# A planned retention and MLP kernel: tile 7's q and k transposed by DMA, one more pair split, TensorE's order changed at the start

## The chip, the cores and the metric

The kernel runs on one core of one Trainium2 chip. The metric is the device time of one execution in microseconds (us), lower is better. The median of four runs of the kernel before is 216.2 us (215.89 to 217.82).

The engines are named as the profile does: PE is TensorE (PEld its weight loads), DVE is VectorE, ACT is ScalarE, POOL is GpSimd and SP is SyncE, which only issues DMAs here.

## The reference

There are 4 sequences of 768 steps with 8 heads of width 64. The first half is a recurrence per head with a decay gamma:

```
gamma = 1 - 2 ** (-5 - h)
for t in range(S):
    state = gamma * state + k[t] (outer) v[t]
    y[t]  = q[t] @ state / sqrt(D)
```

The heads of y are laid side by side, which gives x with 4 x 768 rows of 512. The second half is a normalization and a two-layer network with a residual:

```
xn  = (x - mean(x)) / sqrt(var(x) + 1e-6) * g_ln
out = x + max(xn @ w_ch1, 0) @ w_ch2        # w_ch1: 512 x 2048, w_ch2: 2048 x 512
```

Inputs and output are float32; the kernel computes its products in bf16.

## The kernel before, in words

The 3072 rows are cut into 24 tiles of 128 (`TILES`): tiles 0 to 3 are the first chunks of the four sequences, and then come the other five chunks of each sequence, 4 to 8, 9 to 13, 14 to 18, 19 to 23.

For each tile the recurrence is done chunk by chunk. Its q and k are needed with the head's width on the partitions, so they are transposed, and q is scaled (`trq`). There are two ways. A tile below `T0` is transposed on PE: `e_tk` (L403) and `e_tq` (L410) write four 128x128 blocks each into PSUM (`tp`), ACT copies k's out (`trk`), and DVE scales q's out of PSUM (L415). A tile from `T0` on has q and k loaded into one buffer `qk` (five of them), and SP issues one DMA that transposes both (`tr`, L425); DVE then scales q from SBUF (L432). The PE steps of a tile are: `e_pa` (L442), scores of q and k; DVE multiplies them by the decay mask (`asb`, L449); `e_py` (L461, L465), the state's part and the chunk's part of y; `e_pd` (L511), the chunk's addition to the state, from `vg` (v scaled, on POOL, L498), which DVE turns into the next `state` (L525). DVE takes mean and variance of y (L479, L480) and writes the normalized `xn` (L474), ACT copies y as the residual (`x_all`, L485).

For the network, xn is transposed: below `TX` on PE (L541, copied out by ACT, L188), else by DMA (L555). `GROUPS` says how many tiles share one first product: `e_m1` (L588) multiplies w1 blocks by 1, 2 or 4 tiles' xn (128, 256 or 512 columns), 16 row blocks in all, several in one step so that each step fills a 512-column PSUM tile (`mm`, two of them). ACT or DVE applies the maximum (`h`, L601, L603). `e_m2` (L625) makes the second product of a tile, 16 multiplications of 512 columns in four parts, and DVE adds the residual (`osb`, L633); SP stores it.

The order of everything is set by a small planner (`Plan`) while the kernel is built. Each step is added with an engine, an assumed length, a rank, the steps that it comes after, and the buffer that it takes; `lat` is an assumed extra delay until others see it, and `follows` puts it behind another step in the plan without using its result. `order()` picks again and again the step that can start earliest, then the lowest rank. What it yields is each engine's fixed instruction order; on the chip only that order and the semaphores count, not the planner's times. A changed number in the plan can thus move steps that are not named in the change. `fill` puts products of zeros (L649) into PE's planned gaps in the first 20 us of the plan. Loads are issued by POOL (L342 and L350), cast to bf16 on the way, in its planned order between its `vg` steps, and each load waits for the eighth before it.

The lines that matter here:

```
GROUPS = [1] * 6 + [2] * 5 + [4] * 2
T0, TX = 8, 8
gbm = a(PE, 1000, 2, c_gb, [grd, small2], ("mm", "g"), at=7600)
2800 if kind in "qkv" and j > 7 else 1400 if late(kind, j) else 250,
tk = a(PE, 230, r - 0.1, e_tk, [loaded["k", t], ident] + ([tq] if tq else []),
       ("tp", ("k", t)), [where["k", t]])
```

Of the kernel before, what the change touches and what calls it, by code (L numbers as in the profile page):

```python
# [14 lines left out]
PE, ACT, DVE, POOL, SP = range(5)  # L15
# [101 lines left out]
def kernel(  # L117
# [26 lines left out]
    NPAIR = H // 2  # L144
    TILES = [(b, 0) for b in range(B)] + [(b, c) for b in range(B) for c in range(1, C)]
    number = {bc: t for t, bc in enumerate(TILES)}
    GROUPS = [1] * 6 + [2] * 5 + [4] * 2
    NG = len(GROUPS)
    G0 = [sum(GROUPS[:g]) for g in range(NG)]
    GMAX = max(GROUPS)  # L150
    T0, TX = 8, 8

    buf_of = {g: divmod(G0[g], GMAX) for g in range(NG)}
    group_of = {G0[g] + i: (g, i) for g in range(NG) for i in range(GROUPS[g])}

# [27 lines left out]
    def take(pool, key, shape, dtype):  # L183
        held[pool, key] = pools[pool].tile(shape, dtype, name=pool, tag=pool)
        return held[pool, key]

    def evacuate(eng, dst, src):
        nc.scalar.copy(out=dst, in_=src) if eng == ACT else nc.vector.tensor_copy(out=dst, in_=src)  # L188
# [85 lines left out]
    a = plan.add  # L274
    small = a(DVE, 1450, -100, c_small)
    small2 = a(DVE, 200, -99, c_small2)
# [16 lines left out]
    def c_gb(eng):  # L293
# [2 lines left out]

    grd = a(SP, 390, -150, lambda eng: nc.sync.dma_start(
        out=grow[0:1, :], in_=moe_g_ln.rearrange("(o n) -> o n", o=1)), [small], lat=4500)
    gbm = a(PE, 1000, 2, c_gb, [grd, small2], ("mm", "g"), at=7600)
    gl = a(ACT, 600, -40, lambda eng: nc.scalar.copy(out=gb, in_=held["mm", "g"]), [gbm],  # L300
           uses=[("mm", "g")])

# [2 lines left out]
    loaded, where = {}, {}  # L305

    def tile_of(kind, t):
        if kind != "v" and t >= T0:
            return held["qk", t][:, "qk".index(kind)]
        return held[where[kind, t]]  # L310

    def load(kind, j, rank):
        takes, uses, follows = None, [], []
        if kind in "qkv":
            b, c = TILES[j]
            src = {"q": q, "k": k, "v": v}[kind][b].rearrange("h (c p) d -> c p h d", p=P)[c]
            ns, dma = 910, 900
            pair = kind != "v" and j >= T0
            name = "qk" if pair else kind + ("0" if c == 0 and kind != "q" else "sb")
            takes = where[kind, j] = (name, j)  # L320
            if pair and kind == "q":
                takes, uses, follows = None, [takes], [loaded["k", j]]

            if j == 0:

                def emit32(eng):
                    dst = take("osb", kind, [P, DM], FP32).rearrange("p (h d) -> p h d", d=D)
                    (nc.scalar if eng == ACT else nc.sync).dma_start(out=dst, in_=src)
                raw = a(ACT if kind == "q" else SP, 390, -200 + "kqv".index(kind), emit32, (),
                        ("osb", kind), (), 0, {"k": 3400, "q": 4000, "v": 4800}[kind])  # L330

                def emit(eng):
                    evacuate(eng, take(*takes, [P, H, D], BF16),
                             held["osb", kind].rearrange("p (h d) -> p h d", d=D))
                loaded[kind, j] = a({"k": {ACT: 620}, "q": {DVE: 490}, "v": {ACT: 620, DVE: 430}}[kind], 0, -60, emit,
                                    [raw], takes, [("osb", kind)])
                return

            def emit(eng):
                if takes:  # L340
                    take(*takes, [P, 2, H, D] if pair else [P, H, D], BF16)
                nc.gpsimd.dma_start(out=tile_of(kind, j), in_=src)  # L342
        else:
            s = slice(j * DM, (j + 1) * DM)
            o = slice(j * KO, (j + 1) * KO)
            src, dst = (w1_v[:, :, s], w1[:, :, s]) if kind == "w1" else (w2_v[:, o, :], w2[:, o, :])
            ns, dma = 820, 2450 if kind == "w1" else 2800

            def emit(eng):
                nc.gpsimd.dma_start(out=dst, in_=src)  # L350
        loaded[kind, j] = a(POOL, ns, rank, emit, (), takes, uses, dma,
                            2800 if kind in "qkv" and j > 7 else 1400 if late(kind, j) else 250,
                            follows=follows)

    def late(kind, j):
        return j > 2 if kind in "qkv" else kind == "w2" or j > 0
# [8 lines left out]
    for i, (x, j) in enumerate(seq):  # L365
        load(x, j, pool_rank.get(f"{x}_{j}" if x[0] == "w" else f"{x}{j}", 20 * i))
# [5 lines left out]
    for g in range(NG):  # L372
        for ho in range(HO):
            unit["1", g, ho] = u
            u += GROUPS[g] / 4
            if g >= 6 and (ho + 1) % (HO // GROUPS[g]) == 0 and behind:
                unit["2", behind.pop(0)] = u
# [7 lines left out]
    for t in range(NT):  # L385
        g, i = group_of[t]
# [5 lines left out]
    for t in range(NT):  # L392
        b, c = TILES[t]
        r = rank_of[t]
        g, i4 = group_of[t]
# [3 lines left out]
        if t < T0:  # L399
            def e_tk(eng, t=t):  # L400
                p = take("tp", ("k", t), [P, NPAIR, P], BF16)
                for i in range(NPAIR):
                    nc.tensor.transpose(p[:, i, :], tile_of("k", t)[:, 2 * i:2 * i + 2, :], idn)  # L403
            tk = a(PE, 230, r - 0.1, e_tk, [loaded["k", t], ident] + ([tq] if tq else []),
                   ("tp", ("k", t)), [where["k", t]])

            def e_tq(eng, t=t):
                p = take("tp", ("q", t), [P, NPAIR, P], BF16)
                for i in range(NPAIR):
                    nc.tensor.transpose(p[:, i, :], tile_of("q", t)[:, 2 * i:2 * i + 2, :], idn)  # L410
            tq = a(PE, 230, r, e_tq, [loaded["q", t], ident, tk], ("tp", ("q", t)),
                   [where["q", t]])

            def e_eq(eng, t=t):
                nc.vector.tensor_tensor(out=take("trq", t, [P, NPAIR, P], BF16),  # L415
                                        in0=held["tp", ("q", t)], in1=qsc, op=ALU.mult)
            eq = a(DVE, 430, r, e_eq, [tq, qscd] + ([eq] if eq else []), ("trq", t), [("tp", ("q", t))])

            def e_ek(eng, t=t):
                evacuate(eng, take("trk", t, [P, NPAIR, P], BF16), held["tp", ("k", t)])  # L420
            ek = a({ACT: 590}, 0, r, e_ek, [tk], ("trk", t), [("tp", ("k", t))])
            kt = ("trk", t)
        else:
            def e_tr(eng, t=t):
                nc.sync.dma_start_transpose(  # L425
                    out=take("tr", t, [P, H, P], BF16),
                    in_=held["qk", t].rearrange("p a h d -> p (a h d)"))
            ek = a(SP, 1230, r - 16, e_tr, [loaded["k", t], loaded["q", t]], ("tr", t), [("qk", t)],
                   1500, 5000)

            def e_eq(eng, t=t):
                nc.vector.tensor_tensor(out=take("trq", t, [P, NPAIR, P], BF16),  # L432
                                        in0=held["tr", t][:, 0:NPAIR, :], in1=qsc, op=ALU.mult)
            eq = a(DVE, 490, r, e_eq, [ek, qscd, eq, am], ("trq", t), [("tr", t)])
            kt = ("tr", t)
# [10 lines left out]
        pat = a(PE, 430, r + 1.2, e_pa, [eq, ek], ("pa", t), [("trq", t), kt])  # L446
# [43 lines left out]
        if c > 0:  # L490
            for cc in ([0, 1] if c == 1 else [c]):
                if cc == C - 1:
                    continue
                j = number[b, cc]

                def e_vg(eng, j=j, cc=cc):
# [7 lines left out]
                        follows=[loaded["q", j + 2]] if T0 <= j < NT - 2 else [])  # L504
# [46 lines left out]
        else:  # L551
            def e_ex(eng, t=t, xb=xb, xi=xi):
                if xi == 0:
# [4 lines left out]
                      follows=[ex[t - 1]] if xi else [])  # L558
# [53 lines left out]
    for t, cols in [(t, slice(0, DM)) for t in range(NT - 1)] + [  # L612
            (NT - 1, slice(0, DM - P)), (NT - 1, slice(DM - P, DM))]:
        g, i4 = group_of[t]
# [70 lines left out]
```

## Time and profile before

| | |
|---|---|
| median of four runs | 216.2 us |
| the profiled execution | 217.66 us |
| its span | 215.9 us |
| PE busy | 205.7 us |
| DVE busy | 122.5 us |
| ACT busy | 82.0 us |
| POOL busy | 89.5 us |
| granted TensorE clock | 0.999 |
| read from and written to HBM | 27.27 MB, 6.29 MB |

The span is the time from the first to the last instruction that the profiler saw; the execution's own time is 1.76 us longer. Busy time of an engine is the time in which it worked on at least one instruction. The page gives groups of equal instructions, with the mean length of one. A product's length there is the time through the array, and products overlap, so the spacing of two is less than the mean length; the chain and the timeline give spacings. The chain follows the work that ended last back from the end: at each step to what released it. In the timeline the idle time ahead of an instruction stands in brackets with what ended it.

### The profile page before, as it was taken

Reading aid. Unit: us, or ns where it says so; the run is one execution under the profiler, and the core shown is the slowest. Engines: PE = TensorE matmul, PEld = TensorE weight load, DVE = VectorE, ACT = ScalarE, POOL = GpSimd, SP = SyncE. Lnnn points to the kernel's source line nnn. Section 1 sums busy time; section 2 is a strip of 40 time slices with the busy share of each in tenths; the row PEclk is TensorE's granted clock in tenths of the full one; section 3 lists DMA queues with packets and bytes.
Section 4 is the critical chain, followed back from the end, with each engine's and each line's share of the span. In section 5 each row is a group of like instructions: output and inputs, shape, how many; then the busy total and the mean of one; then the engine's idle time right before and its main releaser. Section 6 shows DMA issues by size and latency. Waiting matters only on the chain.

```text
span 215.9 us, 4578 instructions
## 1 busy us (share of the span) xinstructions
PE 205.7 (95%) x1889; PEld 132.5 (61%) x1911; DVE 122.5 (57%) x233; ACT 82.0 (38%) x153; POOL 89.5 (41%) x105
## 2 busy tenths in 40 slices
PE   7888999999999997899999999999999999999994
PEld 2557999986855645687778775544444444444442
DVE  7695878985148999995776586697011111012121
ACT  5455656674421113255546541136540044430000
POOL 8987779966961839876602930000000000000000
PEclk9999999999999999999999999999999999999999
DMA  7999999999999999999999996412111111011212
GB/s 141 179 179 180 180 157 191 207 163 147 146 158 175 225 140 212 168 162 133 145 149 164 148 182 117 125 24 76 24 49 49 49 49 52 0 49 49 97 52 97
DMA packets 108326, 26.91 MB, mean 125 GB/s; under 512 B 101009, under 2 KB 105361, under 8 KB 108306
## 3 DMA queue, kind: packets, MB, share of 16 engines
q0 software_dynamic: 75984, 13.24, 87.2%
q1 hardware_dynamic: 31138, 13.05, 32.0%
q10 hardware_dynamic: 1184, 0.33, 0.7%
q8 instruction: 15, 0.25, 0.5%
q14 instruction: 5, 0.04, 0.1%
HBM read 27.27 MB, written 6.29 MB: 155 GB/s over the span
## 4 chain that ended last, share of the span: by engine, by line
PE 82%; DVE 9%; DMA 3%; issue 2%; POOL 2%; ACT 1%; POOLq 0%
PE mm L588 38%; PE tp L625 33%; DMA k<-in_k_dram 3%; PE pa L442 3%; DVE asb L449 2%; PE py L465 2%; DVE trq L432 2%; PE py L461 2%; PE pd L511 2%; DVE state L525 1%; DVE osb L633 1%; DVE bns L479 1%; PE tp L541 1%; PE tp L403 1%; PE tp L410 1%
## 5 line engine op out<-in xcount | busy, mean ns | idle before, releaser
L588 PE MATMUL mm<-xnt,w 128*128 128x128 bf16 (+2 forms) x832 | 93.5, 264 | 0.9 <-ACT h L601 0.9
L625 PE MATMUL tp<-w,h 128*128 128x512 bf16 (+2 forms) x380 | 86.5, 370 | 1.5 <-issue 0.6
L588 PEld LDWEIGHTS <-w 128*128 128x128 bf16 x832 | 65.0, 98 | 21.8 <-issue 1.3
L601 ACT ACTIVATE h<-mm 128x512 bf16<-128x512 f32 x89 | 52.7, 597 | 62.5 <-PE mm L588 49.4
L625 PEld LDWEIGHTS <-h 128*128 128x128 bf16 x400 | 37.3, 98 | 39.7
L633 DVE SCALAR_TENSOR_TENSOR osb<-tp,rstd,x_all 128x512 f32<-128x512 f32 (+2 forms) x25 | 18.2, 728 | 58.8 <-PE tp L625 58.6
L449 DVE TENSOR_TENSOR asb<-pa,mask 128x1024 bf16<-128x1024 f32 x24 | 29.3, 1220 | 6.8 <-PE pa L442 6.7
L485 ACT CAST x_all<-py 128x512 bf16<-128x512 f32 x24 | 14.0, 585 | 28.4 <-DVE xn L474 26.5
L479 DVE BATCH_NORM_STATS2 bns<-py 128x6 f32<-128x512 f32 x24 | 16.7, 697 | 12.2 <-PE py L465 12.0
L342 POOL DMA_DIRECT2D qk<-in_k_dram x16 | 14.3, 893 | 17.9 <-DMA tr<-qk 13.2
L498 POOL TENSOR_TENSOR vg<-vsb,vsc 128x512 bf16<-128x512 bf16 x16 | 17.1, 1067 | 7.6 <-DMA vsb<-in_v_dram 7.5
L342 POOL DMA_DIRECT2D vsb<-in_v_dram x20 | 18.4, 918 | 0.5 <-DMA v<-in_v_dram 0.5
L474 DVE SCALAR_TENSOR_TENSOR xn<-py,mv,gb 128x512 bf16<-128x512 f32 x24 | 18.0, 751 | 0.9
L525 DVE TENSOR_TENSOR state<-pd,gch 64x256 bf16<-64x256 f32 x40 | 16.7, 417 | 0.3
L342 POOL DMA_DIRECT2D qk<-in_q_dram x16 | 14.4, 898 | 1.6 <-DMA w<-in_moe_w_ch_dram 1.6
L432 DVE TENSOR_TENSOR trq<-tr,qsc 128x512 bf16<-128x512 bf16 x16 | 9.2, 573 | 5.9 <-DMA tr<-qk 5.6
L649 PE MATMUL mm<-zeros 128*128 128x128 bf16 (+1 forms) x35 | 8.7, 367 | 1.4 <-DVE zeros L221 1.2
L563 ACT ACTIVATE rstd<-mv,epsb 128x1 f32<-128x1 f32 (+2 forms) x13 | 3.5, 294 | 12.7 <-DVE mv L480 12.7
L465 PE MATMUL py<-vsb,asb 128*128 128x64 bf16 x160 | 7.9, 193 | 0.0
L442 PE MATMUL pa<-trq,tr 64*128 64x128 bf16 x128 | 6.4, 218 | 1.6 <-DVE trq L432 1.6
L465 PEld LDWEIGHTS <-asb 128*128 128x128 bf16 x192 | 7.8, 98 | 0.1
L461 PE MATMUL py<-state,trq 128*128 128x128 bf16 x80 | 7.7, 219 | 0.0
(65 smaller groups left out, 112.8 us busy)
## 6 DMA issues: line engine op xcount, KB each, us to landing
out_dram<-osb SPq DMA_DIRECT2D x23, 256.0 KB, 2.0
w<-in_moe_w_ch_dram POOLq DMA_DIRECT2D x8, 512.0 KB, 9.4
vsb<-in_v_dram POOLq DMA_DIRECT2D x20, 128.0 KB, 8.7
qk<-in_k_dram POOLq DMA_DIRECT2D x16, 128.0 KB, 9.1
qk<-in_q_dram POOLq DMA_DIRECT2D x16, 128.0 KB, 9.3
qsb<-in_q_dram POOLq DMA_DIRECT2D x7, 128.0 KB, 8.8
ksb<-in_k_dram POOLq DMA_DIRECT2D x4, 128.0 KB, 9.9
k<-in_k_dram POOLq DMA_DIRECT2D x3, 128.0 KB, 7.2
```

The lines of the kernel that those rows point to most:

```text
L342: nc.gpsimd.dma_start(out=tile_of(kind, j), in_=src)
L449: nc.vector.tensor_tensor(out=take("asb", t, [P, NPAIR, 2, P], BF16).rearrange("p i a t -> p a i t"), in0=held["pa", t], in1=mask.rearrang ...
L465: nc.tensor.matmul(py[:, h, :], lhsT=held["asb", t][:, h // 2, h % 2, :], rhs=tile_of("v", t)[:, h, :], start=(mi == 0), stop=(mi == n - 1))
L474: nc.vector.scalar_tensor_tensor(out=take("xn", t, [P, DM], BF16), in0=held["py", t].rearrange("p h d -> p (h d)"), scalar=mv[:, t, 0:1], ...
L479: nc.vector.bn_stats(out=bns[:, t, :], in_=held["py", t].rearrange("p h d -> p (h d)"))
L485: nc.scalar.copy(out=x_all[:, t, :].rearrange("p (h d) -> p h d", d=D), in_=held["py", t])
L498: e.tensor_tensor(out=take("vg", j, [P, H, D], BF16), in0=tile_of("v", j), in1=vsc[:, cc, :].unsqueeze(2).to_broadcast([P, H, D]), op=ALU. ...
L525: nc.vector.tensor_tensor(out=held["pb", n][o, :, o], in0=held["pd", b][o, :, o], in1=gch[o, cc, :].unsqueeze(2).to_broadcast([D, NPAIR, D ...
L588: nc.tensor.matmul(p[:, j, :], lhsT=w1[:, ko, (ho + j) * P:(ho + j + 1) * P], rhs=held["xnt", hb][:, h0:h0 + n, ko, :], start=(ko == 0), s ...
L601: nc.scalar.activation(out=dst, in_=src, func=AF.Relu)
L625: nc.tensor.matmul(held[key], lhsT=held["h1", hb][:, ho, i * P:(i + 1) * P], rhs=w2[:, ho, cols], start=(ho == 0), stop=(ho == HO - 1))
L633: nc.vector.scalar_tensor_tensor(out=take("osb", key, [P, w], FP32), in0=held[key], scalar=rstd[:, t:t + 1], in1=x_all[:, t, cols], op0=AL ...
```

## The change

The first product's groups become eight single tiles, four pairs and two groups of four. `T0` goes from 8 to 7: tile 7's q and k are loaded into a `qk` buffer and transposed by a DMA from SP instead of on PE. The rank of g's product (which spreads g_ln over the partitions) goes from 2 to 12. The planner's assumed delay of loads is raised for the first loads and for tiles from 8 on. Tile 1's k transposes are planned to start no earlier than the end of tile 0's L442.

```
-    GROUPS = [1] * 6 + [2] * 5 + [4] * 2
+    GROUPS = [1] * 8 + [2] * 4 + [4] * 2
...
-    T0, TX = 8, 8
+    T0, TX = 7, 8
...
-    gbm = a(PE, 1000, 2, c_gb, [grd, small2], ("mm", "g"), at=7600)
+    gbm = a(PE, 1000, 12, c_gb, [grd, small2], ("mm", "g"), at=7600)
...
-                            2800 if kind in "qkv" and j > 7 else 1400 if late(kind, j) else 250,
+                            4000 if kind in "qkv" and j > 7 else 1400 if late(kind, j) else 500,
...
             tk = a(PE, 230, r - 0.1, e_tk, [loaded["k", t], ident] + ([tq] if tq else []),
-                   ("tp", ("k", t)), [where["k", t]])
+                   ("tp", ("k", t)), [where["k", t]],
+                   follows=[pat] if t == 1 else [])
```

In the order that this gives, PE runs tile 0's L442 ahead of tile 1's transposes, g's product behind both of tile 1's transposes, and tile 0's xn transposes (L541) ahead of tile 2's k transposes. Tile 7's scores, y and xn transposes come in PE's list within the second products of tiles 0 to 2, and no longer within the first products of tiles 4 and 5; the steps of tiles 8 to 23 and the second products interleave differently. SP issues tile 7's transpose first. POOL issues the loads of q 8, v 8, k 9 and q 9 ahead of the `vg` steps of tiles 7 and 1. Line numbers of the kernel after are one higher from L406 on.

## The prediction

> **What bounds it now.** I read the page's busy line and its chain first, then PE's groups by form, the chain and the timeline stretch by stretch, and last POOL's and DVE's timelines beside each other.
>
> ```profile
> PE 205.7 (95%) x1889; PEld 132.5 (61%) x1911; DVE 122.5 (57%) x233; ACT 82.0 (38%) x153; POOL 89.5 (41%) x105
> ...
> PE 82%; DVE 9%; DMA 3%; issue 2%; POOL 2%; ACT 1%; POOLq 0%
> ```
>
> PE is the bound; a change pays where it shortens PE's list or takes a hole out of it. Two places have holes. The first is the start, up to the first product of tile 0 (L588); here is the chain in order of time (start, length, what):
>
> ```profile
> 12.18 0.05 issue
> 12.22 0.40 PE tp L403 x4
> 12.62 0.22 PE mm L541 x4
> 12.85 0.22 PE mm L649
> 13.06 0.33 PE tp L410 x4
> 13.39 0.06 PE mm L649
> 13.45 0.32 PE py L465 x8
> 13.77 0.22 PE mm L649
> 13.98 0.95 PE mm L588 x16
> ```
>
> L649 are fillers on zeros. The second is a stretch where the chain runs on DVE (71 to 91 us), which PE's timeline shows with the idle time in brackets, and the chain with its cause:
>
> ```profile
> 86.41 0.40 PE L442 MATMUL pa<-trq,tr 64*128 64x128 bf16 x8 [0.98 <-DVE trq L432]
> ...
> 91.04 0.40 PE L442 MATMUL pa<-trq,tr 64*128 64x128 bf16 x8 [0.60 <-DVE trq L432]
> ```
>
> ```profile
> 84.19 2.08 DVE trq L432
> ...
> 89.92 0.98 DVE trq L432
> ```
>
> The same operation over all tiles (min/median/max ns), and what POOL did then:
>
> ```profile
> L432 DVE TENSOR_TENSOR trq<-tr,qsc x16: 415/426/2080, 56.0 to 144.9; 128x512 bf16<-128x512 bf16 x16
> ```
>
> ```profile
> 84.90 1.07 POOL L498 TENSOR_TENSOR vg<-vsb,vsc 128x512 bf16<-128x512 bf16 x1
> ...
> 89.57 1.04 POOL L498 TENSOR_TENSOR vg<-vsb,vsc 128x512 bf16<-128x512 bf16 x1 [0.99 <-DMA vsb<-in_v_dram]
> ```
>
> Thirteen of sixteen take 0.42 us. The three long ones (0.63 at 56.0, 2.08, 0.97) end 0.28 to 0.30 us after the end of a vg on POOL (55.31 to 56.35, 84.90 to 85.97, 89.57 to 90.61). So the 1.58 us that PE loses before tiles 13 and 14 come from a meeting of trq and vg.
>
> The Trainium skill (SBUF — State Buffer, Who interferes with whom) says that a VectorE operation with both inputs in SBUF contends with a GpSimd operation that reads SBUF, and that the one issued first keeps the port. The three rows agree with the contention; 84.19, where trq began before vg by the trace, does not agree with the order. It speaks against the change: tile 7's trq now reads SBUF, too.
>
> **The start.** (1) L442 of tile 0 stood behind tile 1's k transposes, which waited for k (landed 7.63), and ran at 8.22. Now it waits for trq of tile 0 alone, which DVE ended at 7.52: about 7.6. (2) Tile 1's q transposes come ahead of g's product; q landed at 8.54, so they run at 8.6, then g's product (0.97 from 8.55 to 9.52 before) to 9.8, and L465 of tile 0 at 9.85 for 9.95. That alone is 0.1. (3) asb of tile 0 ends near 9.2 for 9.89, so trq of tile 1 is out of the way earlier; bns of tile 0 starts at 10.1 for 10.39, and xn, then asb of tile 1 end 0.3 earlier, at 11.9 and 13.05. (4) k and q of tile 2 still land at 12.18 and 12.95 and hold their transposes. But tile 0's xn is transposed ahead of them, ACT copies xnt ahead of trk (it ended at 13.83, now near 13.1), and the 0.22 filler at 13.77 goes. L465 of tile 1 follows the q transposes at 13.25, and L588 starts at 13.5 for 13.98. (5) Behind it the fillers are as many, but fewer stand between xn's transposes of tile 1 (15.56, now 15.35) and the second L588 (16.34, now 15.75; its w landed at 15.46). From there to 20.7 the chain alternates L588 and h (L601), so 0.55 is carried on. Bounds: 0, where the landings hold it, and 0.7. I take -0.55, by (5).
>
> **Tile 7 and the groups.** Two times four transposes leave PE: four take 0.22 in the chain, so -0.45. The pair of tiles 6 and 7 becomes two singles: 16 products of 128 columns take 0.89, 16 of 256 take 1.75.
>
> ```profile
> L588 PE MATMUL mm<-xnt,w 128*128 128x256 bf16 x320 | 38.9, 273 | 0.0
> ...
> L588 PE MATMUL mm<-xnt,w 128*128 128x128 bf16 x384 | 24.4, 219 | 0.9 <-ACT h L601 0.9
> ```
>
> The means are latencies, so I take the spacing: 128 x 55.8 ns = 7.14 against 64 x 109.4 = 7.00: +0.14. The h copies are as many (0.60 each, below 0.89). Net -0.3; bounds -0.45 and, if every h of the eight single steps came late like the two 0.45 waits at 17.9 and 19.7, +3.3.
>
> The Trainium skill (TensorE: Matmul & The Clock Gate, Back-to-back issue gap) gives a sustained 81 ns for a load and a product of 128 columns. By that the pair's split would cost 10.4 - 7.0 = 3.4 us, and the change would lose; the chain's 16 in 0.89 us say 56, so I don't use it.
>
> Tile 7's own work comes far later: its L442 moves from 26.9 to 37.3 us into PE's list (counted from the first L588, with the lengths above), some 53.9 us by the clock. Its k and q were issued at 26.50 and 28.61 and landed by 34.7; the q load waited 1.17 for a buffer, which it no longer needs. A transpose by SP took 8.3 in the median and 11.7 at most, so it is there by 47. DVE was nearly idle from 52 to 62. Cost 0.
>
> **The DVE stretch.** Between L442 of tile 8 and of tile 13 PE's list holds 22.8 us before (19 quarters of the second product at 0.86, two L588 steps of 0.88, five each of 0.33 and 0.45, three of 0.22) and 22.8 after (16 quarters, five L588 steps). DVE has four osb (0.75) in both. From asb of tile 8 (62.85) to trq of tile 13 (84.19) DVE needed 21.3, of which 1.3 waiting. So without a long trq DVE stays ahead by 0.4 to 1 us, and the 1.58 us are lost only when vg meets trq in the wrong place. The new order puts these tiles 2.3 to 3.2 us later in PE's list, vg by other landings. My reckoning has vg of tile 15 end near 86.7 and trq of tile 13 start near 86.7: too close to tell. Bounds: -1.6 and +1.6 (every long trq again, and one more). I take -1.6, as thirteen of sixteen are short.
>
> **Queues.** SP gets one transpose more, ahead of all others; tile 12's moves behind tile 8's xnt transpose, and 13's behind a store. POOL issues q8, v8, k9, q9 ahead of vg 7 and vg 1 (two times 1.05 us); vg 7 is ready near 41 and needed near 44. As tile 7 uses one of the five qk buffers, k of tile 12, issued at 53.23, now waits for tile 8's transpose to land, which I put at 58 (55.97 before, and two for tile 7's). Everything behind it on POOL (q 12, vg 10, v 12, k 13) is near 5 us later. q 12 then lands at 69, its transpose is issued at 70, lands at 78.5; trq needs it at 81.8: 3 us spare. Cost 0; without that cover up to 5.
>
> The xnt transposes for the pairs take 6.5 in the median; the tightest, tile 9's, is issued at 73.3 and needed at 82.4. The tail is the same.
>
> **Sum.** 217.66 (the profiled execution, span 215.9) - 0.55 - 0.3 - 1.6 = 215.2. It lies 1.5 above the median of the runs, 216.2, so the forecast is 213.8.
>
> **Rivals.** A, the forecast: 0.50. B, trq meets vg again at one or two tiles: for it, vg waits for v's landing once per tile, as trq follows the same pace; three of 16 did. Only the 0.85 is left: 215.3. Chance 0.30. C, the hole at the start is not closed, as landings hold each step, and B besides: 215.9; chance 0.06. D, slower: k 12's wait on POOL. If transposes in that stretch take the 11.7 of the slowest rather than 8.6, tile 8's lands at 61, q 12 at 72.6, tile 12's transpose at 84.3, 2.5 after it is needed, and tile 13's follows it likewise; DVE and PE stand for 2.5 to 5 us: 216.2 - 0.85 + 3.5 = 218.9. It decides from a lateness of 3 us on. For it: the DMA row of the page is at 9 in every slice from the second to the 24th, to 129 us. Against it: PE needs these tiles 2.7 us later as well. Chance 0.14.
>
> **Numbers.** One per cent is 2.2 us, about what a measurement of this kernel can tell from no change: 214.0 and 218.4. A lies at the edge; I give 0.42 of its 0.50 to below 214.0, as its start term may be 0.7 and gaps of 0.16 may go as well. Faster 0.42, same 0.44 (the rest of A, B, C), slower 0.14. The range takes in A to its best bounds (0.7 + 0.45 + 1.6 and some spread: 212.7) and B and C to the runs' spread above them: 217.0.
>
> **What would show it.** After: first L588 at 13.5, tile 3's L442 (21.82) at 21.2; 128 columns at 56 ns in the new singles; no wait of L442 on trq, and no trq over 0.5 us near tiles 13 and 14; SP's tile 12 transpose near 70. Wrong would be: DVE trq waiting for tr in the sixties to eighties (D), a trq of 1 to 2 us with L442 idle behind it (B), or L588 of the singles idle before an h.

## The result, and the profile after

The kernel after takes 215.61 us in the median (54 executions, 215.33 to 216.3), the kernel before 216.04 us (78 executions). The ratio is 0.9969, with a 95% interval of 0.9961 to 0.9977: faster by 0.3%, where 1.1% was forecast. The medians are 0.43 us (0.2%) apart and the means 0.66, as 13 of the 78 executions before lie above 216.9 us and none of the 54 after does. The time lies in the stated range; the forecast was 1.8 us too low, and case A, which had been given 0.50, did not come.

The profiled execution took 215.53 us, with a span of 213.8 us. It is a typical one. That of before, 217.66 us, was not: it lies 1.6 us above the median of 78. The page's busy line and chain of the kernel after:

```profile
PE 204.6 (96%) x1945; PEld 132.1 (62%) x1966; DVE 121.2 (57%) x235; ACT 80.9 (38%) x152; POOL 89.2 (42%) x105
...
PE 91%; DMA 3%; POOL 2%; issue 1%; DVE 1%; ACT 1%; POOLq 0%
```

The chain ran on DVE for 9% of the span before and does so for 1% now. The stretch from 71 to 91 us has left it: no L443 (L442 before) waits for L433 any more. The same operation over all tiles (durations in ns: min/median/max), from the answer on its line:

```profile
L433 DVE TENSOR_TENSOR trq<-tr,qsc x17: 394/416/899, 47.5 to 144.1; 128x512 bf16<-128x512 bf16 x17
```

Two long ones are left: 0.90 at 73.83, where a `vg` has been at work since 73.40, and 0.70 at 119.86, beside the issue of a load and no `vg`. Nothing waits for either. So far this looks like the gain that was forecast. But the start looks like before. The chain of the kernel after, in order of time (start, length, what):

```profile
13.10 0.05 issue
13.15 0.40 PE tp L411 x4
13.54 0.23 PE py L466 x8
13.78 0.89 PE mm L589 x16
14.67 0.33 PE pa L443 x8
15.00 0.16 issue
15.16 0.55 PE mm L650 x4
15.71 0.36 PE tp L542 x4
16.07 0.17 PE mm L650 x3
16.24 0.91 PE mm L589 x16
```

The filler between L466 and the first L589 is gone, as forecast. But xn's transposes of tile 1 (L542) begin at 15.71, not at the 15.35 of the forecast, the second L589 begins at 16.24, not at 15.75, and behind it the two waits for h (0.45 at 17.82, 0.46 at 19.55) are there as before.

Two distances cut the time in two. The first is from the landing of tile 2's q (12.87 to 13.13 us in these kernels, with the change and without) to tile 3's L442 (L443): 8.87 us before, 8.62 after. The second is from there to the end of PE's last product: 190.93 us in the profiled execution of before, 188.99 after. The experiments below say which of these two differences belong to the change.

### The profile page after: what moved, and what is told of

Its sections match the earlier page's. It is cut to its first block, busy times and chain, and to the rows that moved or that the text cites. A ratio compares the mean times of both kernels' runs of the same rounds, so it can differ in the third digit from the quotient of the medians.

```text
span 213.8 us, 4698 instructions
## 1 busy us (share of the span) xinstructions
PE 204.6 (96%) x1945; PEld 132.1 (62%) x1966; DVE 121.2 (57%) x235; ACT 80.9 (38%) x152; POOL 89.2 (42%) x105
## 4 chain that ended last, share of the span: by engine, by line
PE 91%; DMA 3%; POOL 2%; issue 1%; DVE 1%; ACT 1%; POOLq 0%
PE mm L589 40%; PE tp L626 39%; PE pa L443 3%; DMA qsb<-in_q_dram 3%; PE py L466 2%; PE pd L512 2%; PE py L462 2%; POOL k L342 1%; PE tp L542 1%; ACT h L602 1%; PE tp L411 0%; POOL qsb L342 0%; POOL v L342 0%; PE tp L403 0%; POOL w L350 0%
## 5 line engine op out<-in xcount | busy, mean ns | idle before, releaser
L589 PE MATMUL mm<-xnt,w 128*128 128x128 bf16 (+2 forms) x896 | 93.7, 257 | 0.9 <-ACT h L602 0.9
L589 PEld LDWEIGHTS <-w 128*128 128x128 bf16 x896 | 65.8, 98 | 19.6 <-issue 1.1
L342 POOL DMA_DIRECT2D qk<-in_k_dram x17 | 15.2, 892 | 14.1 <-DMA tr<-qk 11.4
L342 POOL DMA_DIRECT2D qk<-in_q_dram x17 | 15.2, 893 | 3.0 <-DMA w<-in_moe_w_ch_dram 3.0
L650 PE MATMUL mm<-zeros 128*128 128x128 bf16 (+1 forms) x34 | 7.6, 347 | 1.5 <-DVE zeros L221 1.2
L433 DVE TENSOR_TENSOR trq<-tr,qsc 128x512 bf16<-128x512 bf16 x17 | 7.8, 461 | 0.6 <-DMA tr<-qk 0.6
L466 PEld LDWEIGHTS <-asb 128*128 128x128 bf16 x192 | 7.9, 98 | 0.3 <-DVE trq L416 0.3
L462 PEld LDWEIGHTS <-trq 128*128 128x128 bf16 x80 | 6.0, 98 | 3.2
L466 PE MATMUL py<-vsb,asb 128*128 128x64 bf16 x160 | 7.9, 193 | 0.0
```

The costliest lines, as they stand in the source:

```text
L462: nc.tensor.matmul(py[:, 2 * i:2 * i + 2, :], lhsT=held["trq", t][:, i, :], rhs=held["pb", t][:, i, :], start=(mi == 0), stop=False)
L466: nc.tensor.matmul(py[:, h, :], lhsT=held["asb", t][:, h // 2, h % 2, :], rhs=tile_of("v", t)[:, h, :], start=(mi == 0), stop=(mi == n - 1))
L589: nc.tensor.matmul(p[:, j, :], lhsT=w1[:, ko, (ho + j) * P:(ho + j + 1) * P], rhs=held["xnt", hb][:, h0:h0 + n, ko, :], start=(ko == 0), s ...
```

## Experiments

### The kernel before, profiled once more (b1)

The same kernel, unchanged.

> The kernel before, unchanged, to see another execution. Theory 1 (the two holes of 0.98 and 0.60 us ahead of L442 of tiles 13 and 14 belong to the one execution that was profiled, 217.66 us, and not to most): about 216.0 us, span 214.2, trq (L432) at most 0.6 us near 84 and 90 us, no idle time of L442 on trq. Theory 2 (the holes are in every execution, and the change lost its gain elsewhere): the holes of together 1.6 us are there again, and the span beside a time of 216.0 can't be 215.9.

Measured: 216.07 us, ratio 1.0013 [0.9995, 1.0031]; the profiled execution took 215.93 us, span 214.2. VectorE's timeline of this execution, at the place where the first profile had its 2.08 and 0.98:

```profile
84.18 0.42 DVE L432 TENSOR_TENSOR trq<-tr,qsc 128x512 bf16<-128x512 bf16 x1
...
88.26 0.43 DVE L432 TENSOR_TENSOR trq<-tr,qsc 128x512 bf16<-128x512 bf16 x1
```

Both are short, and no L442 waits for them. GpSimd's timeline of the same execution:

```profile
83.97 0.90 POOL L342 DMA_DIRECT2D qk<-in_q_dram  x1
84.86 1.07 POOL L498 TENSOR_TENSOR vg<-vsb,vsc 128x512 bf16<-128x512 bf16 x1
...
88.76 1.04 POOL L498 TENSOR_TENSOR vg<-vsb,vsc 128x512 bf16<-128x512 bf16 x1 [0.21 <-PE tp L625]
```

The first `vg` comes right behind the q load's issue, as in the first profile, 0.04 us earlier, and yet the outcome is another. From tile 3's L442 to the end are 189.24 us here, against 190.93 with the holes. The second long trq of the first profile may follow from the first: it began at 89.92, 1.66 us later than here, and so within a `vg` (89.57 to 90.61), while here trq is ahead of it. So the 1.6 us belong to the execution that was profiled and not to most: 217.66 - 1.6 = 216.06 is the kernel's median, and of the 90 executions of this kernel timed beside the experiments two come near 217.66 at a clock of 1.00 (216.98 and 217.41). A kernel that lost the holes for good could gain next to nothing on that median.

### The two edits at the start alone (start_only)

```diff
-    gbm = a(PE, 1000, 2, c_gb, [grd, small2], ("mm", "g"), at=7600)
+    gbm = a(PE, 1000, 12, c_gb, [grd, small2], ("mm", "g"), at=7600)
...
-                   ("tp", ("k", t)), [where["k", t]])
+                   ("tp", ("k", t)), [where["k", t]],
+                   follows=[pat] if t == 1 else [])
```

> Before, with only the two edits at the start (rank of g's product 12, tile 1's k transposes behind L442 of tile 0); PE's order is the old one from L442 of tile 2 on. Theory 1: xn of tile 1 waits for the landing of q of tile 2, as before, so 0 to 0.2 us are gained (ratio 0.999 to 1.000). Theory 2 (as predicted): 0.55 us, ratio 0.9975.

Measured: 215.96 us, ratio 0.9996 [0.9984, 1.0008]. Tile 3's L443 comes 8.84 us after tile 2's q, as in the kernel before (8.84 in b1). The edits that name the start bring nothing that shows, and the interval leaves no room for the 0.55 us of the forecast.

### Everything but these two (rest_only)

The kernel after with the two edits above taken back:

```diff
-    gbm = a(PE, 1000, 12, c_gb, [grd, small2], ("mm", "g"), at=7600)
+    gbm = a(PE, 1000, 2, c_gb, [grd, small2], ("mm", "g"), at=7600)
...
-                   ("tp", ("k", t)), [where["k", t]],
-                   follows=[pat] if t == 1 else [])
+                   ("tp", ("k", t)), [where["k", t]])
```

> After, with the two edits at the start undone; groups, T0 and the planner's load delays as after. Theory 1: the 0.3 us of the shorter list, ratio 0.9985, and what the start gives is missing (0.1 to 0.2 above the kernel after). Theory 2: 0.55 above the kernel after, ratio about 0.9995.

Measured: 215.52 us, ratio 0.9975 [0.9961, 0.9989]: the whole gain of the change, without the edits at the start. It has the same two distances as after, 8.62 and 188.99 us. So the shorter first distance comes from something else that the change holds.

### The planner's delay of the first loads alone (early_lat)

```diff
-                            2800 if kind in "qkv" and j > 7 else 1400 if late(kind, j) else 250,
+                            2800 if kind in "qkv" and j > 7 else 1400 if late(kind, j) else 500,
```

> Before, with only the planner's delay of the first loads raised from 250 to 500. On PE this puts tile 0's xn transposes ahead of tile 2's k transposes and takes one 512-column filler (0.22 us) out from between tile 1's xn transposes and the second L588. Theory 1 (L442 of tile 3 follows the landing of tile 2's q by 8.84 us in before and in the kernel with the start's two edits alone, by 8.62 in after and in the kernel with the rest alone): 8.62 here, so 0.2 us and a ratio of 0.999. Rival (the 0.2 comes from the split or from tile 7): 8.84 and 1.000.

Measured: 215.66 us, ratio 0.9982 [0.9964, 1.0]. The first distance is 8.62 us, the second 189.25, as in b1. TensorE's timeline of this kernel, with tile 0's xn transposes (L541) ahead of tile 2's k (L403) and the filler in front of the first L588 gone:

```profile
12.04 0.40 PE L541 MATMUL mm<-idn,xn 128*128 128x128 bf16 x4 [0.66 <-DVE xn L474]
12.28 0.39 PE L403 MATMUL tp<-idn,k 128*128 128x128 bf16 x4
...
13.26 0.40 PE L465 MATMUL py<-v,asb 128*128 128x64 bf16 x8
13.49 1.06 PE L588 MATMUL mm<-xnt,w 128*128 128x128 bf16 x16
...
15.55 0.40 PE L541 MATMUL tp<-idn,xn 128*128 128x128 bf16 x4
15.79 0.33 PE L649 MATMUL mm<-zeros 128*128 128x128 bf16 x3
15.95 1.06 PE L588 MATMUL mm<-xnt,w 128*128 128x128 bf16 x16
```

The first L588 comes 0.51 us behind the landing, against 0.81 in b1, but that is not where the 0.22 us lie. Tile 1's xn transposes, which wait for VectorE's xn, begin at 15.55 here and in b1, 2.57 us behind the landing in both. The gain is right behind them. In the old order a filler of 512 columns stands there beside the three of 128, as the timeline of groups_t0 (below, with the start of the kernel before) shows:

```profile
15.70 0.40 PE L541 MATMUL tp<-idn,xn 128*128 128x128 bf16 x4
15.94 0.55 PE L649 MATMUL mm<-zeros 128*128 128x512 bf16 x4
16.32 1.06 PE L588 MATMUL mm<-xnt,w 128*128 128x128 bf16 x16
```

From xn's transposes to the second L588 are 0.62 us there, as in b1, and 0.40 here. An assumed delay that stands for nothing on the chip moved the steps: 0.22 us, the length of that one filler.

### T0 alone, and T0 with the groups (t0_only, groups_t0)

```diff
-    T0, TX = 8, 8
+    T0, TX = 7, 8
```

> Before, with only T0 = 7 (tile 7's q and k transposed by DMA, groups as before). Theory 1: PE's list is 0.45 us shorter and PE hardly stands elsewhere, so ratio 0.998. Rival: the later tiles' transposes and loads are held back by tile 7's place among the qk buffers, and DVE waits for tr: ratio 1.000 or more.

Measured: 216.63 us, ratio 1.0024 [1.0, 1.0048]: no gain, rather a loss. TensorE's timeline of this kernel shows three waits that before doesn't have:

```profile
46.76 0.38 PE L511 MATMUL pd<-vg,k 128*128 128x128 bf16 x4 [0.52 <-DVE state L525]
...
59.34 1.02 PE L625 MATMUL tp<-w,h 128*128 128x512 bf16 x4 [0.50 <-DVE osb L633]
...
71.61 0.40 PE L442 MATMUL pa<-trq,tr 64*128 64x128 bf16 x8 [0.52 <-DVE trq L432]
```

The last follows a trq of 1.31 us at 70.15 that met a `vg` at 70.14: in this execution three waits of 0.5 eat the transposes' 0.45 and more. It took 217.28 us, 0.65 above the median of its eleven, so a typical one need not have all three. VectorE waited only 0.3 us for transposes, so the reason that the rival gave is not what shows. With the groups of after besides:

```diff
-    GROUPS = [1] * 6 + [2] * 5 + [4] * 2
+    GROUPS = [1] * 8 + [2] * 4 + [4] * 2
...
-    T0, TX = 8, 8
+    T0, TX = 7, 8
```

> Before, with the groups and T0 of after, and the planner's delays and the start's edits as before. Theory 1: PE's list is 0.3 us shorter; if nothing stands in the later order, ratio 0.9985, with L442 of tile 3 at 8.84 behind tile 2's q. Rival (T0 = 7 holds the later tiles back whatever the groups, as it did alone with 1.5 us of holes in PE): 1.002 or more; then it is the raised delays of the later loads that close the holes in after.

Measured: 215.82 us, ratio 0.9982 [0.996, 1.0004]. The first distance is that of before, 8.84 us; the second is 189.15, in which one wait of 0.27 stands, so PE's list is 0.36 shorter than b1's 189.24 (189.15 - 0.27 = 188.88). So the split pair seems to pay not by its own length but by the places that it makes for tile 7's steps. Half of tile 7's own first product, in the chain of the kernel after (its L443 ran at 54.25), is as fast as the old singles were:

```profile
61.63 1.79 PE mm L589 x32
```

That is 55.9 ns for a product of 128 columns. The Trainium skill (TensorE: Matmul & The Clock Gate, Back-to-back issue gap) gives 81 ns for a sustained load and product; the measurement decides against it here.

### The fillers behind 12.4 us taken out (after_nofill, rest_nofill)

The start of after still has fillers ahead of xn's transposes and waits for h behind the second L589, as its timeline shows:

```profile
17.82 1.05 PE L589 MATMUL mm<-xnt,w 128*128 128x128 bf16 x16 [0.45 <-ACT h L602]
...
19.55 1.05 PE L589 MATMUL mm<-xnt,w 128*128 128x128 bf16 x16 [0.46 <-ACT h L602]
```

The products of zeros are written into an `mm` buffer, of which there are two.

```diff
-        for t in plan.fill(plan.order(), PE, 1100, 20000, lambda at: 110 if at < 11500 else 80, warm):
+        for t in plan.fill(plan.order(), PE, 1100, 12400, lambda at: 110 if at < 11500 else 80, warm):
```

> After, without the fillers on zeros behind 12.4 us of the plan. Two L588 steps of tile 1 wait 0.45 us each for h at 17.8 and 19.6 us. Theory: the fillers keep one of the two mm buffers until 20.7 us, so that each step waits for the copy of the step ahead; without them both waits go and the fillers' own time, so 0.9 to 1.5 us, ratio to before 0.991 to 0.994. Rival: the waits stay (they come from ACT's length), or the granted clock falls with the fillers gone: at most 0.2 us against after, or slower.

Measured: 214.69 us, ratio 0.9942 [0.9929, 0.9955], the best kernel of this study. TensorE's timeline of it:

```profile
15.45 0.40 PE L542 MATMUL tp<-idn,xn 128*128 128x128 bf16 x4 [0.67 <-DVE xn L475]
15.68 1.06 PE L589 MATMUL mm<-xnt,w 128*128 128x128 bf16 x16
...
16.82 1.06 PE L589 MATMUL mm<-xnt,w 128*128 128x128 bf16 x16
...
17.94 1.06 PE L589 MATMUL mm<-xnt,w 128*128 128x128 bf16 x16
...
20.11 0.40 PE L443 MATMUL pa<-trq,trk 64*128 64x128 bf16 x8 [0.44 <-DVE trq L416]
```

The two waits for h are gone (L589 is idle ahead of none of the three), and tile 3's L443 stands 7.23 us behind tile 2's q instead of 8.62. Of this 1.39 us, 0.45 goes back when a k load that PE now waits for lands at 23.04; the span is 1.0 us shorter in the profiled executions (213.8 and 212.8, of which an earlier landing of q makes 0.2), the median 0.9. The start of this kernel is thus held by the fillers more than by what the change moves. That they did it through the `mm` buffers is read from the row's name and the waits that went with them, not tested by itself.

The same edit on rest_only, as a second pair:

> After with the start's two edits undone and without the fillers behind 12.4 us of the plan. Theory 1 (these two edits bring nothing): as the kernel after without fillers, 214.7 us, ratio to before 0.994. Rival: 0.2 to 0.5 above it.

Measured: 214.92 us, ratio 0.9928 [0.9902, 0.9954], against 0.9975 for rest_only (215.52 us). The gain comes again without the edits at the start. It lies 0.23 us above after_nofill, at the lower edge of the rival's range, but the executions overlap (214.51 to 215.26 here, 214.46 to 215.16 there): whether the two edits bring 0.2 us once the fillers are gone stays open.

### Tile 2's loads ahead of w1's first quarter (q2_early_nofill)

On top of after_nofill:

```diff
-    first = ["iota", "pos", "k1", "q1", "v1", "w1_0", "k2", "q2", "w1_1", "v2", "k3", "q3", "v3",
+    first = ["iota", "pos", "k1", "q1", "v1", "k2", "q2", "w1_0", "w1_1", "v2", "k3", "q3", "v3",
```

> The kernel after without those fillers, and with tile 2's k and q loaded ahead of the first quarter of w1. Theory (the start hangs on the landing of tile 2's q, 12.9 to 13.1 us): q lands near 11.2 and w1 near 13, so the first L588 comes at 13.2 and tile 1's xn earlier: 0.3 to 1 us under the kernel without fillers. Rival: w1's first quarter, now later, holds L588, and nothing is gained or up to 0.5 lost.

Measured: 214.93 us, ratio 0.9951 [0.9938, 0.9963]; nothing gained. Tile 2's q lands at 10.92 instead of 12.88, but TensorE's timeline shows that the next thing is late right behind it:

```profile
12.98 0.41 PE L466 MATMUL py<-v,asb 128*128 128x64 bf16 x8 [0.73 <-DVE asb L450]
13.22 1.06 PE L589 MATMUL mm<-xnt,w 128*128 128x128 bf16 x16
```

Tile 1's xn transposes come at 15.18 instead of 15.45, but the q of tile 3 now holds TensorE for 0.29 us at 19.29, and tile 3's L443 is at 20.20, against 20.11. The landing that I had taken for the wall of the start is one of two at the same place; the other is VectorE's chain of tiles 0 and 1.

### What trq pays when it meets GpSimd (meet_alone, meet_forced, meet_earlier)

First the price by itself: copies of trq on spare tiles near the end of the kernel before, four at a time, first with GpSimd idle, then beside 16 operations like `vg` back to back, then beside memsets of GpSimd. They are work that is added; nothing is left out.

```diff
+                for i in range(4):
+                    nc.vector.tensor_tensor(out=dout, in0=dsrc, in1=qsc, op=ALU.mult)
...
+                    for i in range(16 if tile_no == 16 else 1):
+                        nc.gpsimd.tensor_tensor(
+                            out=pout, in0=x, in1=vsc[:, 0, :].unsqueeze(2).to_broadcast([P, H, D]),
+                            op=ALU.mult)
+                    for i in range(20 if tile_no == 20 else 0):
+                        nc.gpsimd.memset(pout, 0.0)
```

> Before, with trq's operation (128x512 bf16, both inputs in SBUF) added 36 times on DVE on spare tiles, four behind each osb of tiles 14 to 22, where POOL has nothing else to do: beside an idle POOL (tiles 14, 15), beside sixteen of vg's operation in a row on POOL (from tile 16), and beside one vg and twenty memsets of POOL (from tile 20). Theory (vg holds trq up): 0.42 us beside the idle POOL and beside the memsets, 0.8 to 1.3 beside vg. Rival (the long trq has another cause, such as the loads' descriptors): 0.42 everywhere.

Measured in one execution: VectorE's timeline, four copies to a row; GpSimd idle at 173.67, its products from 181.28 to 199.80, its memsets from 204.90 to past 212:

```profile
173.67 1.79 DVE L674 TENSOR_TENSOR dout<-dsrc,qsc 128x512 bf16<-128x512 bf16 x4
...
181.12 3.90 DVE L674 TENSOR_TENSOR dout<-dsrc,qsc 128x512 bf16<-128x512 bf16 x4
...
206.62 1.79 DVE L674 TENSOR_TENSOR dout<-dsrc,qsc 128x512 bf16<-128x512 bf16 x4
```

Alone one copy takes 0.42 us. Beside GpSimd's products it takes 1.15; only the first of each row differs, and the one at 181.12, which began before them, kept 0.36. Beside memsets it is 0.42 again. The Trainium skill (SBUF — State Buffer, Who interferes with whom) says just this: two inputs from SBUF contend with a GpSimd operation that reads SBUF, not with one that only writes, and the one issued first keeps the port. This run agrees, with 0.42 against 1.15.

Next the meeting in its place: a GpSimd operation that reads the state as soon as VectorE has written it, for tiles 12 and 13.

```diff
+            if t.get("tile") in (12, 13):
+                nc.gpsimd.tensor_tensor(
+                    out=pout, in0=held["pb", t["tile"]].rearrange("p i (a d) -> p (i a) d", d=D),
+                    in1=vsc[:, 0, :].unsqueeze(2).to_broadcast([P, H, D]), op=ALU.mult)
```

> Before, with one more of vg's operation on POOL for tiles 12 and 13 each, that reads the state which DVE writes just ahead of trq, so that it starts as trq starts, and trq meets it in every execution. Theory (a long trq on these tiles is what makes the holes ahead of L442, and most executions of before have none): trq of tiles 12 and 13 about 1.0 to 1.5 us, L442 idle behind them, 0.4 to 1.8 us over before (ratio 1.002 to 1.008). Rival (the holes come from something else in the execution that was profiled): trq long, but the time as before.

Measured: 216.44 us, ratio 1.0018 [0.9993, 1.0043], and the meeting did not come about as meant. GpSimd's operations began at 80.96 and 85.76, VectorE's trq at 80.91 and 85.65, a little earlier: trq kept its 0.43, and GpSimd's operation took 1.27 and 1.21. So at the two places this run says nothing on what a late trq costs, but again that the first to start keeps the port. Four other trq of this execution began within a `vg` and took 1.30, 1.24, 1.23 and 1.77 us; of these only the one at 89.73 left TensorE idle, for 0.28 us. A long trq costs what VectorE lacks at that place, and often nothing.

Last, the same operation half as wide and released by the first half of the state, so that GpSimd is at work when trq starts, for tiles 11 to 14:

```diff
+                        if o.start == 0 and n in (11, 12, 13, 14):
+                            nc.gpsimd.tensor_tensor(
+                                out=pout[0:D],
+                                in0=held["pb", n][0:D].rearrange("p i (a d) -> p (i a) d", d=D),
+                                in1=vsc[0:D, 0, :].unsqueeze(2).to_broadcast([D, H, D]), op=ALU.mult)
```

> The kernel before, with one added GpSimd operation (a copy of 64 partitions of the state row, 1024 elements, released when the first half of that row is written) for tiles 11 to 14. It begins about 0.43 us ahead of trq, the product of t and rq on VectorE, so that trq starts while GpSimd already reads. Theory 1 (long trqs ahead of L442 make the holes that the profiled execution of before had): trq takes about 0.9 us for these four tiles instead of 0.43, 4 x 0.48 = 1.9 us of VectorE's time, of which some 0.6 us is spare, so about +1.3 us: 217.3 us, ratio 1.006, with holes of TensorE ahead of L442 that end on trq. Theory 2 (a long trq alone costs nothing, since the later meetings of b1, 0.77 and 1.20 us, left no hole): within 0.2 per cent of before, no hole that ends on trq.

Measured: 223.26 us, ratio 1.0297 [1.0243, 1.0351]. TensorE's timeline of this kernel:

```profile
81.98 0.40 PE L443 MATMUL pa<-trq,tr 64*128 64x128 bf16 x8 [0.85 <-DVE trq L433]
...
87.28 0.40 PE L443 MATMUL pa<-trq,tr 64*128 64x128 bf16 x8 [0.60 <-DVE trq L433]
...
94.27 0.40 PE L443 MATMUL pa<-trq,tr 64*128 64x128 bf16 x8 [2.96 <-DVE trq L433]
```

The four trq took 0.92, 2.07, 0.97 and 3.31 us in place of 0.43 each: 5.55 us more, of which 4.41 reach PE as holes; the first left none. The rest, 1.1 us, is what VectorE had spare. So Theory 1 holds in kind, a long trq ahead of L442 makes the hole, and its size was far off, as two of the four took two to four times the 0.9 that I had given them.

## Why the prediction was right or wrong

**The sum** is where it failed, at the term of the DVE stretch. It takes 1.6 us off the profiled execution's 217.66 for the holes, and then a further 1.5 because that execution lies 1.5 above the median. These are the same 1.6 us: b1 shows the kernel before at 215.93 without the holes. By the median the DVE stretch was worth 0, and the other two terms at their measured size give 216.04 - 0.22 - 0.25 = 215.57, against 215.61 measured. That it comes so close is in part luck, as single executions with the same order differ by 0.1 us and more.

**The DVE stretch, -1.6:** the mechanism was right in kind, as meet_earlier shows: trq is held while GpSimd reads, L442 waits, and after has no such wait. The term was not, since a meeting that comes or stays away when trq begins at 84.19 or 84.18 and `vg` at 84.90 or 84.86 is no fixed cost of a kernel. "Thirteen of sixteen are short" was used for the kernel after alone; it held for before as well. (The addends of PE's list give 22.7 us on both sides, not 22.8; that the two are equal stands.)

**The start, -0.55:** 0.22 came (8.84 to 8.62). Steps (1) to (3) came close to their numbers: L443 of tile 0 ran at 7.58, L466 of tile 0 at 9.80, xn of tile 0 ended at 12.02 (forecast 11.9) and asb of tile 1 at 13.15 (13.05). But this is hardly the change's doing, as xn ended at 12.07 and asb at 13.21 in b1, with the old order. Step (4) came: the first L589 begins 0.51 us after q's landing, where the forecast has 0.55 and b1 0.81 (timelines: 13.61 behind 13.10, 13.79 behind 12.98). Step (5), by which I chose the value, failed in its first half. It has tile 1's xn transposes 0.21 us earlier, and they came 2.57 us behind the landing as in b1, as VectorE's timeline of the kernel after shows:

```profile
13.58 0.42 DVE L416 TENSOR_TENSOR trq<-tp,qsc 128x512 bf16<-128x512 bf16 x1 [0.43 <-PE tp L411]
13.92 0.69 DVE L480 BATCH_NORM_STATS2 bns<-py 128x6 f32<-128x512 f32 x1
...
14.87 0.75 DVE L475 SCALAR_TENSOR_TENSOR xn<-py,mv,gb 128x512 bf16<-128x512 f32 x1
```

The trq of tile 2 stands ahead of tile 1's bns and xn and waits for the transposes (L411) of tile 2's q. So xn of tile 1 ends at 15.62, where it ended at 15.51 before. Without that trq at most 0.14 us would be won: bns needs L466, which stands behind the same transposes on PE and ended at 13.78, and bns began at 13.92. The landing that I let hold step (4) holds step (5) too. Its second half, fewer fillers ahead of the second L588, came as one filler: 0.22 us (0.62 to 0.40 from xn's transposes to the second product, by the timelines) for a forecast 0.38. And the edit that brought the 0.22 was the planner's delay of the first loads (early_lat), not the two that name the start (start_only).

**Tile 7 and the groups, -0.3:** right, as far as single executions tell. The second distance is 188.99 us against 189.24 in b1, -0.25; in groups_t0 it is -0.36 without its one wait. In start_only, with the order of before in this part, it is 189.10, so 0.1 us is scatter. The spacing of 56 ns held in tile 7's single, and no L589 of the new singles waited for an h. What the sum by edits hides is that T0 alone loses 0.2% (t0_only).

**Queues, 0:** right. GpSimd's timeline of after shows k 12 waiting for tile 8's transpose:

```profile
58.40 0.87 POOL L342 DMA_DIRECT2D qk<-in_k_dram  x1 [2.28 <-DMA tr<-qk]
```

58 was the forecast; SP issued tile 12's transpose at 70.95 (forecast 70), and it landed at 76.36 (forecast 78.5). Tile 7's own landed at 47.51 (forecast: by 47). VectorE waited 0.6 us in all for transposes, and rival D had nothing to show.

**Rivals:** B (215.3) and C (215.9) both lie 0.3 us from the time. They count holes from trq's meeting with vg as still there, which the profile of after refutes; their numbers come close because they leave the holes alone in a sum made on the median. What C says of the start, that landings hold it, is in part what came. No rival said that the median had no holes; a second profile of the kernel before would have told.

## What to carry to other kernels

If the profiled execution lies above the median by about as much as the holes that it shows, the holes may belong to that execution alone: set the sum against the median, and take from it only what a typical execution loses. An engine's step that waits for a landing also holds every step that stands behind it in its order, so look there before you carry a gain past it. A step that comes earlier is worth nothing while the next one waits for something else: here the 0.3 us gained at the first L588 were lost again ahead of xn's transposes. Fillers are work like any other: here those behind 12.4 us of the plan cost 0.9 us, perhaps by the buffer that they take.

## What the hardware showed that was not expected

**A late trq waits for more than one operation.** In meet_earlier two of the four ended 0.28 to 0.29 us after GpSimd's reading operation (0.92 and 0.97), as in the profile of before. The longest, on VectorE's timeline:

```profile
90.81 3.31 DVE L433 TENSOR_TENSOR trq<-tr,qsc 128x512 bf16<-128x512 bf16 x1
```

and GpSimd's timeline of the same time:

```profile
90.47 1.03 POOL L530 TENSOR_TENSOR pout<-state,vsc 64x512 bf16<-64x512 bf16 x1 [1.85 <-DVE state L526]
91.46 0.94 POOL L343 DMA_DIRECT2D qk<-in_q_dram  x1
92.42 1.05 POOL L499 TENSOR_TENSOR vg<-vsb,vsc 128x512 bf16<-128x512 bf16 x1
93.41 0.94 POOL L343 DMA_DIRECT2D vsb<-in_v_dram  x1
```

It lasted through the operation, the issue of a load and the `vg` behind it, to 94.12. The one of 2.07 also lasted through an operation and a load's issue. That may be how the 2.08 of before came about, which began during a load's issue (84.01 to 84.90) and ended 0.30 us after the `vg` behind it; but trq in b1 began in the same place and took 0.42. And the 0.70 of after, at 119.86, lies beside a load's issue alone (119.76 to 120.65). What decides between them stays open.

**A long pause of PE can cost twice.** Of meet_earlier's 6.5 us of longer span (against b1), the holes are 4.4. The stretches after the 2.96 us hole, with the engines' busy time (and instructions), then PE's granted clock, the DMA share and GB/s:

```profile
94.00:96.00 2.00, 1.73 (x15) 1.25 (x16) 1.90 (x5) 0.24 (x1) 2.00 (x3) 0.67 1.10 70
96.00:98.00 2.00, 2.00 (x12) 1.38 (x10) 1.99 (x4) 1.13 (x3) 2.00 (x3) 0.50 1.29 177
98.00:100.00 2.00, 2.00 (x18) 1.41 (x17) 0.70 (x4) 0.63 (x2) 2.00 (x4) 0.97 1.83 140
```

The grant falls to 0.67 and 0.50: (0.33 + 0.50) x 2 = 1.7 us more, as much as 3.4 us at half the clock. The other five executions have a mean clock of 0.984 to 0.992, but for the fastest (221.06 us, 0.999). The Trainium skill (TensorE: Matmul & The Clock Gate, Why this matters for your kernels) warns of pauses over about 3 us; here 2.96 was enough. The start of a kernel can meet it as well: in meet_forced's profiled execution, with a pause of 0.91 us at 7.6, the grant was 0.60 from 8 to 12 us and the first product came 1.5 us late, while b1, with 0.87 at the same place, kept 1.00. None of the 110 timed executions of the kernels with a changed start (after, start_only, rest_only, early_lat, after_nofill, rest_nofill and q2_early_nofill) has a mean clock below 0.998; of the kernel before 14 of 102 have 0.992 (three of them b1's, at 217.3 to 217.6 us). Which of the edits does that, and whether the pause near 7.6 us is what decides, was not tried.
